# Batch 0 of a packed-attention and top-1 expert kernel: softmax work shared by VectorE and GpSimd, half of the keys loaded through ScalarE's queue, and new conditions on when second-layer weight casts, weight packs and the last softmax steps may go

## The chip, the cores and the metric

The kernel runs on one core of a Trainium2 chip. The metric is device time of one launch in microseconds (us), the median of several runs; smaller is better. TensorE (PE) does the matrix products, VectorE (DVE), ScalarE (ACT) and GpSimd (POOL) the rest, and SyncE (SP) asks for most transfers.

## The reference, cut to what matters

```python
scale = 1.0 / np.sqrt(q.shape[-1])                 # q, k, v: 8 x 8 x 576 x 64, p: 8 x 8 x 32 x 64
p_packed = sm_attn(p, k, v)                        # 32 packed rows for each head
out = sm_attn(q, p_packed, p_packed)               # softmax over 32 columns
x = out.transpose(0, 2, 1, 3).reshape(B, S, 512)
for b in range(B):
    prev_e = -1
    for s in range(S):
        fresh_e = argmax(x[b, s] @ w_gate)
        e = fresh_e if s == 0 or sigmoid(x[b, s] @ w_local) < 0.5 else prev_e
        prev_e = e
        h = np.maximum(x[b, s] @ w1[e], 0.0)       # w1: 8 x 512 x 1024
        out[b, s] = p[e] * (h @ w2[e])             # w2: 8 x 1024 x 512
```

## The kernel before

There are eight batches. For each one the kernel computes 32 packed rows for every head (scores L447 and L508, exponentials L556, their transposes L567, the product with the values L598), and then, for all 576 rows, the second softmax and the two expert layers. The result of the second attention is never formed: the packed rows are multiplied into w1 first ("pack", L1076), and the softmax of the queries is the moving operand of layer 1 (L1104). Which expert a batch uses is only known after its gate products (L922, L930) and a chain on VectorE (L937, L945, L948, L952, L957) that ends in an expert number (L852); SyncE reads it and then asks for that expert's w1 (two transfers of 1 MB into `w1t`, L1026) and w2 (L1033).

Everything is fp32 split into a high and a low part, so that three products replace one. The high part of a packed weight is a cast on ScalarE (`wph`, L1085), the low part a subtraction on VectorE (`wpl`, L1088). The softmax has `a2h` (L788, ScalarE) and its rest `a2l` (L797); w2 has a cast on ScalarE (L1132) and a rest on GpSimd (L1136), both in `w2s`; the hidden layer has a relu on ScalarE (L1115) and a rest on VectorE (L1119). Layer 1 takes eight chunks of 128 hidden columns, c0 to c7, and for each chunk two parts of the 576 rows, of 256 and of 320. A block is six L1104 products for one part of a chunk, followed by six L1156 products of layer 2 for the same part; L1162 and L1166 take the last 64 rows.

Batch 0 is special ("early" in the code). Its keys and queries come in whole transfers (`load_whole`, L291), and its softmax is made by `first_queries`, in two halves of the columns, z = 0 (256 columns) and z = 1 (320 columns), for two row groups Q0 and Q1. A half goes: transposes (L749), maximum (L755), subtraction (L760), exponential (L762), sum (L767), a small addition (L769), reciprocal (L771), product (L773), transposes back into `a2t` (L781), cast (L788), rest (L797). Until there is enough other work PE runs products on zeros (L227) to stay busy.

The order of the program is not written down. A planner at build time (`weave`) holds threads (loads, scores, packs, splits, softmax, gates) and a main thread with the two layers. It carries an estimate of every engine's time, and at each step it lets the first thread go whose inputs it believes to be ready. Each engine then runs its instructions in that fixed order. A changed condition in batch 0 therefore moves instructions of later batches too, because estimates and the planner's credit differ from there on.

Of the kernel before, what the change touches and what calls it, by code (L numbers as in the profile page):

```python
# [14 lines left out]
ALU = mybir.AluOpType  # L15
# [5 lines left out]
NP = 32  # L21
DM, F, E = 512, 1024, 8
HQ = 4
NQ = H // HQ
NG, NM = 6, 3
# [147 lines left out]
def packed_attn_moe_kernel(  # L173
# [12 lines left out]
    nc = tc.nc  # L186
# [4 lines left out]
    clock = Clock()  # L191
    at_batch = [-1]

    def tile_(shape, dtype, name, tag=None):
        bufs = BUFS.get(tag or name, 2)
        x = sb.tile(shape, dtype, name=name, tag=tag or name, bufs=bufs)
        clock.follow(x.tensor.name, tag or name, bufs)
        return x
# [82 lines left out]
        ready.banks = banks  # L281
        return ready

    def load_whole(src, b):

        x = tile_([128, NG, NM * 2 * D], F32, "raw", "qn")
        clock.edges[x.tensor.name] = (H * HALF // 2,)
        clock.rate = 400.0
        rows = src[b].rearrange("h s d -> (h s d)").rearrange("(p g x) -> p g x", p=128, g=NG)
        for z in (slice(0, NG // 2), slice(NG // 2, NG)):  # L290
            nc.sync.dma_start(out=x[:, z], in_=rows[:, z])  # L291
        return x

    def load_values(src, b, Q, x=None, most=True, ends=True):
# [44 lines left out]
    def load_packs_whole(b, queue):  # L339

        x = tile_([128, NQ, 2, D], F32, "p_in")
        clock.rate = 200.0
        queue.dma_start(out=x[:, :, 0], in_=at(p, b).rearrange("(g h) n d -> (h n) g d", g=NQ))
        return x
# [9 lines left out]
    def loads(st):  # L354

        b = st["b"]
        if st["early"]:
            st["p"] = load_packs_whole(b, nc.sync)
            nc.scalar.activation(out=spare_col, in_=ones_col, func=AF.Exp)
            order = (("k", 0), ("t", 0), ("v", 0), ("v", 1), ("w", 0), ("q", 0))  # L360
        else:
            if isinstance(b, int):
                yield need(when=lambda: "loaded" in sts[b - 1] and (b < 2 or "ereg" in sts[b - 2]) and (b <= FIRST or len(sts[b - 2].get("w2", ())) == NC))
            order = (("e", 0), ("p", 1), ("k", 1), ("v", 0), ("v", 1), ("q", 1)) if st["whole"] else (("v", 0), ("v", 1), ("p", 1), ("k", 1), ("q", 1))
        ends = None
        for name, Q in order:
# [27 lines left out]
            x = {"k": k, "v": v, "q": q}[name]  # L394
# [325 lines left out]
    def first_queries(st):  # L720
# [12 lines left out]
        sT, sf, mx, sm = [], [], [], []  # L733
        for lo, hi, room in parts:
            sT.append(tile_([128, NQ, 2, hi - lo, NP], F32, "sT0", room))
            sf.append(sT[-1].rearrange("a q r m n -> a (q r m) n"))
            n = NQ * 2 * (hi - lo)
            mx.append(tile_([128, n], F32, f"mx{n}"))
            sm.append(tile_([128, n], F32, f"sm{n}"))

        def wide(z, x):
            return x[z].unsqueeze(2).broadcast_to([128, sf[z].shape[1], NP])
# [20 lines left out]
            st["raised"] += 1  # L763

        def shared(z):
            yield need(sT[z])
            nc.vector.reduce_sum(out=sm[z], in_=sf[z], axis=AX.X)  # L767
            yield need(sm[z])
            nc.vector.tensor_scalar(out=sm[z], in0=sm[z], scalar1=1e-9, scalar2=None, op0=ALU.add)  # L769
            yield need(sm[z])  # L770
            nc.vector.reciprocal(out=sm[z], in_=sm[z])  # L771
            yield need(sm[z])
            nc.vector.tensor_tensor(out=sf[z], in0=sf[z], in1=wide(z, sm), op=ALU.mult)  # L773

        def returned(z):
            lo, hi, _ = parts[z]
            cols = slice(64 * lo, 64 * hi)
            yield need(sT[z])
            for Q in range(NQ):
                for r in range(2):  # L780
                    nc.vector.transpose(  # L781
                        out=st["a2t"][Q][:, cols].rearrange("a (m r) -> a r m", r=2)[:, r],
                        in_=sT[z][:, Q, r].rearrange("a m n -> a (m n)"),
                    )
                if Q == NQ - 1:
                    st["back" if z == 0 else "returned"] = True
                yield need(st["a2t"][Q][:, cols])
                nc.scalar.copy(out=st["a2h"][Q][:, cols], in_=st["a2t"][Q][:, cols])  # L788
            st["cast"] = True
            give(sT[z])  # L790
# [15 lines left out]
        yield from turned(1, (0,))  # L806
        yield from shared(0)
        yield from returned(0)
        yield from rest(0, (nc.vector, nc.vector))
        yield from turned(1, (1,))  # L810
        yield from highest(1)
        yield from raised(1)
# [235 lines left out]
    def pack_weights(st):  # L1048

        st["wp"], st["packed"], early = [], 0, st["early"]  # L1050
        for fh in range(2):
            yield need(when=lambda: len(st.get("w1", ())) > fh and (
                (st["seconds"] > 2 if early else st["firsts"] > 0) if fh else not early or st["raised"] > 0
            ))
            pieces = st["w1"][fh]
            yield need(slot=("wph", "wpl"))
# [6 lines left out]
            for n, w1t in enumerate(pieces):  # L1063
# [3 lines left out]
                    yield need(w1t)  # L1067
                    yield from look_for_strays()
                if early:
                    yield need(when=lambda: st["asked"] >= 512 * fh + width * (n + 1) and (n == 0 or st["seconds"] > 0))  # L1070
                yield need(w1t, banks=NQ, skip=skip, left=1)
                ts = [bank(skip=skip) for Q in range(NQ)]
                for Q in range(NQ):
# [66 lines left out]
    def splits(st):  # L1140

        for c in range(NC):
            yield need(slot="w2s", when=lambda: len(st.get("w2", ())) > c and st["firsts"] > (c if st["early"] else c - 3))
            yield need(st["w2"][c])
            yield from split(st, c, 2 if st["early"] and c < FRONT else 1)

# [319 lines left out]
```

## Time and profile before

| quantity | value |
|---|---|
| runs | 411.37, 412.01, 412.96 us, median 412.01 |
| profiled execution | 413.25 us, of which the span from first to last instruction is 411.5 us |
| granted TensorE clock, mean | 0.998 |
| PE busy | 401.1 us, 97% of the span |
| DVE, ACT, POOL busy | 248.1, 187.7, 110.9 us |

The span is the stretch from the first to the last instruction; 1.75 us of the profiled execution lie around it. PE is busy nearly all the time, and the last 11.5 us hold 6.00 us of PE work, with the clock at 0.92 of full speed. In the rows below a number in brackets is idle time of that engine just before the instruction, with what ended it.

### The profile page before, as it was taken

What the parts mean: (1) busy time and instruction counts of PE and PEld (TensorE: products, weight loads), DVE (VectorE), ACT (ScalarE), POOL (GpSimd) and SP (SyncE); (2) the same over time, 40 slices, a digit from 0 to 9 for tenths busy, and PEclk for the clock granted to TensorE, in tenths of its full rate; (3) what the DMA queues carried; (4) which work ended last, traced back from release to release, by engine and by line L of the source; (5) the groups of instructions that cost most, each with busy time, mean ns of one, the idle gap of its engine ahead of it and who ended that gap; (6) DMA issues with size and microseconds to landing.
All of it is one profiled execution on the core that took longest, in us unless ns stands there. A gap on an engine that the chain in (4) does not pass through costs nothing.

```text
span 411.5 us, 9811 instructions
## 1 busy us (share of the span) xinstructions
PE 401.1 (97%) x3726; PEld 318.7 (77%) x3727; DVE 248.1 (60%) x665; ACT 187.7 (46%) x447; POOL 110.9 (27%) x139
## 2 busy tenths in 40 slices
PE   8999999999999999999999999999989999999994
PEld 6766777787787888678887887778868788778883
DVE  3678778673986668568944697248843586332221
ACT  2565535653346533475344643545335643453121
POOL 1024502621064203044304411323303423143000
PEclk9999999999999999999999999999999999999999
DMA  7889589965799199659996994899165102921102
GB/s 231 244 309 246 91 210 357 158 163 131 270 231 241 26 218 183 220 192 211 192 317 204 193 193 142 310 210 213 64 243 168 51 14 64 346 70 48 53 0 68
DMA packets 161053, 72.98 MB, mean 177 GB/s; under 512 B 131186, under 2 KB 139882, under 8 KB 161002
## 3 DMA queue, kind: packets, MB, share of 16 engines
q1 hardware_dynamic: 160858, 72.19, 67.8%
q8 instruction: 30, 0.49, 0.5%
q14 instruction: 21, 0.17, 0.1%
q10 hardware_dynamic: 144, 0.13, 0.1%
HBM read 62.87 MB, written 9.44 MB: 176 GB/s over the span
## 4 chain that ended last, share of the span: by engine, by line
PE 89%; DVE 4%; DMA 3%; ACT 1%; issue 1%; SPq 1%; POOL 0%; DVEq 0%; ACTq 0%
PE bank L1156 42%; PE bank L1104 24%; PE bank L1076 4%; PE bank L1162 4%; PE bank L1166 3%; PE bank L598 2%; PE bank L567 2%; PE bank L647 2%; DMA w2raw<-in_moe_w_dram 2%; DMA w1t<-in_moe_w_dram 2%; PE bank L227 2%; PE bank L922 1%; PE bank L439 1%; PE bank L508 1%; PE bank L616 1%
## 5 line engine op out<-in xcount | busy, mean ns | idle before, releaser
L1156 PE MATMUL bank<-w2s,h 128*128 128x512 f32 (+1 forms) x771 | 203.8, 397 | 0.2 <-POOL w2s L1136 0.2
L1156 PEld LDWEIGHTS bank<-w2s,h 128*128 128x128 f32 x771 | 136.2, 188 | 31.1 <-issue 7.8
L1136 POOL TENSOR_TENSOR w2s<-w2raw,w2s 128x512 fp32r<-128x512 f32 (+1 forms) x68 | 84.6, 1258 | 140.0 <-ACT w2s L1132 118.2
L1119 DVE SCALAR_TENSOR_TENSOR h<-bank,h 128x256 fp32r<-128x256 f32 x192 | 61.8, 350 | 94.3 <-ACT h L1115 93.5
L1115 ACT ACTIVATE h<-bank 128x320 fp32r<-128x320 f32 (+1 forms) x128 | 52.9, 413 | 102.9 <-PE bank L1104 100.0
L1104 PEld LDWEIGHTS bank<-a2h,wph 128*128 128x128 f32 x256 | 46.1, 188 | 17.8 <-issue 3.8
L1104 PE MATMUL bank<-a2h,wph 128*128 128x256 f32 (+1 forms) x256 | 56.9, 303 | 0.1
L1104 PE MATMUL bank<-a2h,wpl 128*128 128x256 f32 (+1 forms) x256 | 55.1, 295 | 1.1 <-DVE wpl L1088 1.1
L1104 PE MATMUL bank<-a2l,wph 128*128 128x256 f32 (+1 forms) x256 | 55.2, 296 | 0.0
L1104 PEld LDWEIGHTS bank<-a2h,wpl 128*128 128x128 f32 x256 | 41.1, 188 | 1.5 <-DVE wpl L1088 1.5
L1104 PEld LDWEIGHTS bank<-a2l,wph 128*128 128x128 f32 x256 | 41.0, 188 | 0.3
L710 POOL TENSOR_TENSOR a2l<-a2t,a2h 128x320 fp32r<-128x320 f32 (+1 forms) x26 | 20.7, 819 | 73.5 <-ACT a2h L704 73.5
L1132 ACT CAST w2s<-w2raw 128x512 fp32r<-128x512 f32 x64 | 39.0, 620 | 1.4 <-DMA w2raw<-in_moe_w_dram 1.3
L1088 DVE TENSOR_TENSOR wpl<-bank,wph 128x512 fp32r<-128x512 f32 (+1 forms) x34 | 21.2, 650 | 21.2 <-ACT wph L1085 21.1
L1085 ACT CAST wph<-bank 128x512 fp32r<-128x512 f32 (+1 forms) x34 | 17.4, 565 | 27.4 <-PE bank L1076 27.2
L1162 PE MATMUL bank<-w2s,h 128*128 128x512 f32 x64 | 26.5, 414 | 0.0
L1166 PE MATMUL bank<-w2s,h 128*64 128x512 f32 x64 | 25.2, 393 | 0.0
L1197 ACT ACTIVATE o<-bank,pe 128x512 f32<-128x512 f32 x23 | 15.5, 698 | 9.3 <-PE bank L1156 9.3
L634 DVE STREAM_TRANSPOSE qn<-qn 128x1152 f32<-128x1152 f32 x14 | 19.1, 1366 | 0.0
L1076 PE MATMUL bank<-w1t,ppT 64*32 64x512 f32 x240 | 16.4, 601 | 1.1 <-DMA w1t<-in_moe_w_dram 1.1
L556 ACT ACTIVATE a<-a,nb 128x576 f32<-128x576 f32 x14 | 11.0, 786 | 13.3 <-DVE nb L536 13.3
L1162 PEld LDWEIGHTS bank<-w2s,h 128*128 128x128 f32 x64 | 12.0, 188 | 6.0 <-issue 2.2
(150 smaller groups left out, 387.2 us busy)
## 6 DMA issues: line engine op xcount, KB each, us to landing
w2raw<-in_moe_w_dram SPq DMA_DIRECT2D x64, 256.0 KB, 7.5
w1t<-in_moe_w_dram SPq DMA_DIRECT2D x15, 1024.0 KB, 5.1
kv<-in_v_dram SPq DMA_DIRECT2D x16, 560.0 KB, 8.7
qn<-in_q_dram SPq DMA_DIRECT2D x28, 288.0 KB, 4.3
out_dram<-o SPq DMA_DIRECT2D x31, 256.0 KB, 2.9
qn<-in_k_dram SPq DMA_DIRECT2D x24, 288.0 KB, 4.3
raw<-in_k_dram SPq DMA_DIRECT2D x4, 576.0 KB
raw<-in_q_dram SPq DMA_DIRECT2D x2, 576.0 KB
```

What stands on the lines that cost most here:

```text
L634: nc.vector.transpose(out=qT, in_=qT)
L710: engine.tensor_tensor(out=a2l[:, cols], in0=a2t[:, cols], in1=a2h[:, cols].bitcast(F32), op=ALU.subtract)
L1076: nc.tensor.matmul(out=ts[Q][32 * h:32 * h + 32, :width], lhsT=st["ppT"][Q][rows, 32 * h:32 * h + 32], rhs=w1t[rows, h], start=True, stop= ...
L1088: nc.vector.tensor_tensor(out=lo[:, Q, cols], in0=ts[Q][:, :width], in1=hi[:, Q, cols].bitcast(F32), op=ALU.subtract,)
L1104: nc.tensor.matmul(out=t[:, :width], lhsT=st["wp"][c // 4][wi][:, Q, fs], rhs=a2[ai][Q][:, ts], start=(n == 0), stop=(n == 5),)
L1115: nc.scalar.activation(out=h[:, :n], in_=t[:, :n], func=AF.Relu)
L1119: nc.vector.scalar_tensor_tensor(out=h[:, dst:dst + z - a], in0=t[:, a:z], scalar=0.0, in1=h[:, a:z].bitcast(F32), op0=ALU.max, op1=ALU.su ...
L1132: nc.scalar.copy(out=w[:, 0], in_=raw)
L1136: rest.tensor_tensor(out=w[:, 1, cols], in0=raw[:, cols], in1=w[:, 0, cols].bitcast(F32), op=ALU.subtract)
L1156: nc.tensor.matmul(out=acc[:, cols], lhsT=hs[hi], rhs=w[:, wi, cols], start=(c == 0 and n == 0), stop=(n == 2 and (c == NC - 1 or c == NC ...
L1162: nc.tensor.matmul(out=acc, lhsT=h[:, EDGE:EDGE + 2 * TAIL], rhs=w[:, 0], start=(c == 0), stop=False, skip_group_check=True,)
L1166: nc.tensor.matmul(out=acc[0:TAIL], lhsT=h[:, EDGE:EDGE + TAIL], rhs=w[:, 1], start=False, stop=(c == NC - 1), skip_group_check=True,)
```

## The change

It has five parts. The first half of batch 0's keys is asked for on ScalarE's queue, and the second half stays on SyncE's. In softmax half z = 0 the product is split: VectorE makes Q0's and GpSimd Q1's, and the planner's clock is told that the tile has two regions; the transposes of a row group then wait for that group only, and Q0's rest goes to GpSimd. The sum and what follows it in half z = 1 wait until more than 512 packed columns are done. The second of the early weight packs waits for two layer-1 blocks instead of one layer-2 block, and in the other batches the second half's pack waits for two chunks instead of one. The w2 casts of batch 0 are released by layer-2 progress from c2 on, and c0's by the softmax cast.

```diff
     def load_whole(src, b, queues=(nc.sync, nc.sync)):
...
-        for z in (slice(0, NG // 2), slice(NG // 2, NG)):
-            nc.sync.dma_start(out=x[:, z], in_=rows[:, z])
+        for queue, z in zip(queues, (slice(0, NG // 2), slice(NG // 2, NG))):
+            queue.dma_start(out=x[:, z], in_=rows[:, z])
...
             st["p"] = load_packs_whole(b, nc.sync)
+            st["rawk"] = load_whole(k, b, (nc.scalar, nc.sync))
             nc.scalar.activation(out=spare_col, in_=ones_col, func=AF.Exp)
-            order = (("k", 0), ("t", 0), ("v", 0), ("v", 1), ("w", 0), ("q", 0))
+            order = (("t", 0), ("v", 0), ("v", 1), ("w", 0), ("q", 0))
...
             sT.append(tile_([128, NQ, 2, hi - lo, NP], F32, "sT0", room))
+            clock.edges[sT[-1].tensor.name] = (2 * (hi - lo) * NP,)
...
         def shared(z):
-            yield need(sT[z])
+            yield need(sT[z], when=lambda: z == 0 or st["packed"] > 512)
             nc.vector.reduce_sum(out=sm[z], in_=sf[z], axis=AX.X)
...
-            nc.vector.tensor_tensor(out=sf[z], in0=sf[z], in1=wide(z, sm), op=ALU.mult)
+            if z:
+                nc.vector.tensor_tensor(out=sf[z], in0=sf[z], in1=wide(z, sm), op=ALU.mult)
+                return
+            n = sf[z].shape[1] // NQ
+            for Q, engine in enumerate((nc.vector, nc.gpsimd)):
+                rows, w = slice(n * Q, n * Q + n), wide(z, sm)
+                engine.tensor_tensor(out=sf[z][:, rows], in0=sf[z][:, rows], in1=w[:, rows], op=ALU.mult)
 
         def returned(z):
...
-            yield need(sT[z])
             for Q in range(NQ):
+                yield need(sT[z][:, Q])
                 for r in range(2):
...
-        yield from rest(0, (nc.vector, nc.vector))
+        yield from rest(0, (nc.gpsimd, nc.vector))
...
             yield need(when=lambda: len(st.get("w1", ())) > fh and (
-                (st["seconds"] > 2 if early else st["firsts"] > 0) if fh else not early or st["raised"] > 0
+                (st["seconds"] > 2 if early else st["firsts"] > 1) if fh else not early or st["raised"] > 0
             ))
...
                 if early:
-                    yield need(when=lambda: st["asked"] >= 512 * fh + width * (n + 1) and (n == 0 or st["seconds"] > 0))
+                    yield need(when=lambda: st["asked"] >= 512 * fh + width * (n + 1) and (n == 0 or st["firsts"] > 1))
...
         for c in range(NC):
-            yield need(slot="w2s", when=lambda: len(st.get("w2", ())) > c and st["firsts"] > (c if st["early"] else c - 3))
+            yield need(slot="w2s", when=lambda: len(st.get("w2", ())) > c and (
+                (st["firsts"] > c if c < 2 else st["seconds"] > c - 2) if st["early"] and c else "cast" in st if st["early"] else st["firsts"] > c - 3
+            ))
```

The change moves instructions. Lines of the changed kernel are one larger from L291 on, two larger around L749 to L762, eight larger around L797 to L1136, and ten larger from L1156 on.

On GpSimd the first place is the work of batch 0 after its last preparation for the scores. Before, the w2 rests of c0 to c3 came in halves, then c4, and then the softmax rest of half z = 1 for Q0 (`a2l`):

```order
L493 MEMSET a_473 128x4
L1136 TENSOR_TENSOR w2s<-w2raw,w2s 128x256 x8
L1136 TENSOR_TENSOR w2s<-w2raw,w2s 128x512
L797 TENSOR_TENSOR a2l<-a2t,a2h 128x320
L1136 TENSOR_TENSOR w2s<-w2raw,w2s 128x512 x2
L493 MEMSET a_723 128x4
L1136 TENSOR_TENSOR w2s<-w2raw,w2s 128x512
```

After it, softmax work of half z = 0 leads, and the rest of half z = 1 for Q0 stands behind all the w2 rests:

```order
L494 MEMSET a_473 128x4
L781 TENSOR_TENSOR sT_417<-sT_417,sm_419 128x256
L805 TENSOR_TENSOR a2l<-a2t,a2h 128x256
L1144 TENSOR_TENSOR w2s<-w2raw,w2s 128x256 x8
L1144 TENSOR_TENSOR w2s<-w2raw,w2s 128x512 x4
L805 TENSOR_TENSOR a2l<-a2t,a2h 128x320
```

On ScalarE at the end of batch 0, from the softmax casts of half z = 1 on, `a` holds the scores of batch 1 and `a1T` their transposes. Before:

```order
L788 CAST a2h<-a2t 128x320
L1115 ACTIVATE h<-bank_665 128x256
L1132 CAST w2s<-w2raw 128x512
L556 ACTIVATE a_473,s_691<-a_473,nb 128x576
L1115 ACTIVATE h<-bank_680 128x256
L1132 CAST w2s<-w2raw 128x512
L1115 ACTIVATE h<-bank_741 128x256
L569 COPY a1T<-bank_770 116x384
L569 COPY a1T<-bank_775 116x256
L556 ACTIVATE a_723,s_784<-a_723,nb 128x576
L965 ACTIVATE ex<-under 128x40
L967 ACTIVATE fresh_all<-lt 128x5
```

After; the relu of the first 320-row block (`bank_759`) and both exponentials now stand ahead of all copies of `a1T`:

```order
L1123 ACTIVATE h<-bank_694 128x256
L796 CAST a2h<-a2t 128x320
L1140 CAST w2s<-w2raw 128x512
L796 CAST a2h<-a2t 128x320
L1123 ACTIVATE h<-bank_759 128x320
L557 ACTIVATE a_473,s_784<-a_473,nb 128x576
L557 ACTIVATE a_741,s_786<-a_741,nb 128x576
L570 COPY a1T<-bank_790 116x384
L570 COPY a1T<-bank_795 116x256
L570 COPY a1T<-bank_806 116x384
L973 ACTIVATE ex<-under 128x40
```

The second place is the border between batches 2 and 3, first on PE, up to the pack (`w1t`) that needs batch 3's expert. Before:

```order
L1156 MATMUL bank_2318<-w2s,h 128x512 x3
L1162 MATMUL bank_2324<-w2s,h 128x512
L1166 MATMUL bank_2324<-w2s,h 64x512
L1104 MATMUL bank_2553<-a2h,wph 128x320 x2
L1104 MATMUL bank_2553<-a2h,wpl 128x320 x2
L1104 MATMUL bank_2553<-a2l,wph 128x320 x2
L567 MATMUL bank_2562<-ident,a_2492 116x128 x3
L567 MATMUL bank_2568<-ident,a_2492 116x128 x2
L1156 MATMUL bank_2311<-w2s,h 128x512 x3
L1156 MATMUL bank_2318<-w2s,h 128x512 x3
L1076 MATMUL bank_2591<-w1t,ppT 32x512 x4
L1076 MATMUL bank_2592<-w1t,ppT 32x512 x4
```

After; the six layer-1 and six layer-2 products between the scores of batch 4 (L508, now L509) and the pack are gone from there:

```order
L1166 MATMUL bank_2307<-w2s,h 128x512 x3
L1166 MATMUL bank_2314<-w2s,h 128x512 x3
L509 MATMUL bank_2546<-qn,p_in 32x288 x4
L509 MATMUL bank_2547<-qn,p_in 32x288 x4
L509 MATMUL bank_2556<-qn,p_in 32x288 x4
L509 MATMUL bank_2557<-qn,p_in 32x288 x4
L1172 MATMUL bank_2319<-w2s,h 128x512
L1176 MATMUL bank_2319<-w2s,h 64x512
L568 MATMUL bank_2581<-ident,a_2540 116x128 x3
L568 MATMUL bank_2586<-ident,a_2540 116x128 x2
L1084 MATMUL bank_2595<-w1t,ppT 32x512 x4
L1084 MATMUL bank_2596<-w1t,ppT 32x512 x4
```

Further ahead, the six layer-1 products of one block and three of layer 2 now stand before the gate products (L922, now L930), where they had stood behind them. On VectorE, from the transpose of the gate's result (`lt`) to the expert's number (`e`). Before:

```order
L937 STREAM_TRANSPOSE lt<-bank_2403 128x160
L945 TENSOR_REDUCE gmx<-lt 128x5
L948 TENSOR_TENSOR under<-lt,gmx 128x40
L460 STREAM_TRANSPOSE qn<-qn 128x4x288
L1119 SCALAR_TENSOR_TENSOR h<-bank_2424,h 128x256
L1119 SCALAR_TENSOR_TENSOR h<-bank_2424,h 128x64
L952 SCALAR_TENSOR_TENSOR vc<-under,code 128x40
L957 TENSOR_REDUCE codes_all<-vc 128x5
L852 TENSOR_SCALAR e_2457<-codes_all 1x1
```

After; one more pair of hidden-layer rests and the transpose of `p_in`, which stood ahead of the gate before, now lie between:

```order
L945 STREAM_TRANSPOSE lt<-bank_2414 128x160
L1127 SCALAR_TENSOR_TENSOR h<-bank_2399,h 128x256
L1127 SCALAR_TENSOR_TENSOR h<-bank_2399,h 128x64
L953 TENSOR_REDUCE gmx<-lt 128x5
L461 STREAM_TRANSPOSE qn<-qn 128x4x288
L956 TENSOR_TENSOR under<-lt,gmx 128x40
L1127 SCALAR_TENSOR_TENSOR h<-bank_2445,h 128x256
L1127 SCALAR_TENSOR_TENSOR h<-bank_2445,h 128x64
L960 SCALAR_TENSOR_TENSOR vc<-under,code 128x40
L423 STREAM_TRANSPOSE p_in<-p_in 128x256
L965 TENSOR_REDUCE codes_all<-vc 128x5
L860 TENSOR_SCALAR e_2468<-codes_all 1x1
```

## Rows read from the trace of the kernel before

**Rows 1.** The page's busy times: us, share of the span, instructions.
```profile
PE 401.1 (97%) x3726; PEld 318.7 (77%) x3727; DVE 248.1 (60%) x665; ACT 187.7 (46%) x447; POOL 110.9 (27%) x139
```

**Rows 2.** Timeline of the first 8 us: start, duration, engine, line, operation.
```profile
1.31 4.63 PE L227 MATMUL bank<-warm 128*128 128x256 f32 x10 [1.31 <-DVE warm L220]
...
1.38 0.94 SPq L291 DMA_DIRECT2D raw<-in_k_dram  x2
```

**Rows 3.** Timeline, 24.5 to 29 us: first softmax half.
```profile
25.06 0.69 DVE L773 TENSOR_TENSOR sT<-sT,sm 128x512 f32<-128x512 f32 x1
```

**Rows 4.** Timeline, 29 to 40 us: two layers of batch 0.
```profile
34.19 0.43 PE L1156 MATMUL bank<-w2s,h 128*128 128x512 f32 x1
...
36.14 1.09 PE L1076 MATMUL bank<-w1t,ppT 64*32 64x512 f32 x16
...
37.16 1.65 PE L1156 MATMUL bank<-w2s,h 128*128 128x512 f32 x6
...
38.65 0.40 PE L1104 MATMUL bank<-a2h,wph 128*128 128x256 f32 x2
...
39.69 0.38 PE L1104 MATMUL bank<-a2h,wpl 128*128 128x256 f32 x1 [0.52 <-DVE wpl L1088]
```

**Rows 5.** Waits of PE, whole span: engine, line, waited for, total, times, longest.
```profile
PE bank L1104 <- DVE wpl L1088: 1.1, 2, 0.6
PE bank L1076 <- DMA w1t<-in_moe_w_dram: 1.1, 1, 1.1
```

**Rows 6.** Timeline, 42 to 52 us: GpSimd beside VectorE, end of batch 0.
```profile
42.24 2.79 POOL L1136 TENSOR_TENSOR w2s<-w2raw,w2s 128x512 fp32r<-128x512 f32 x2
42.32 1.56 DVE L797 TENSOR_TENSOR a2l<-a2t,a2h 128x320 fp32r<-128x320 f32 x1
...
46.60 0.71 PE L567 MATMUL bank<-ident,a 128*116 128x128 f32 x5
...
47.06 0.54 PE L1104 MATMUL bank<-a2h,wph 128*128 128x320 f32 x2
...
49.32 0.75 ACT L569 COPY a1T<-bank 116x384 f32<-116x384 f32 x2
...
51.41 0.96 PE L1156 MATMUL bank<-w2s,h 128*128 128x512 f32 x3
```

**Rows 7.** Timeline, 161 to 178 us: from batch 3's gate to its first layer.
```profile
161.54 0.43 DVE L422 STREAM_TRANSPOSE p_in<-p_in 128x256 f32<-128x256 f32 x1
...
162.29 0.65 PE L922 MATMUL bank<-a2t,gate 128*32 128x128 f32 x16
...
165.34 0.39 PE L1162 MATMUL bank<-w2s,h 128*128 128x512 f32 x1
...
165.80 0.46 PE L1104 MATMUL bank<-a2h,wph 128*128 128x320 f32 x2
...
166.68 0.86 PE L1156 MATMUL bank<-w2s,h 128*128 128x512 f32 x3
...
167.35 1.01 SPq L1026 DMA_DIRECT2D w1t<-in_moe_w_dram  x2
167.41 0.56 DVE L1119 SCALAR_TENSOR_TENSOR h<-bank,h 128x256 fp32r<-128x256 f32 x2 [0.73 <-ACT h L1115]
...
167.47 1.20 PE L508 MATMUL bank<-qn,p_in 64*32 64x288 f32 x32
...
169.51 0.78 ACT L556 ACTIVATE a<-a,nb 128x576 f32<-128x576 f32 x1 [2.13 <-DVE nb L536]
...
172.79 1.09 PE L1076 MATMUL bank<-w1t,ppT 64*32 64x512 f32 x16
...
177.52 0.39 PE L1104 MATMUL bank<-a2h,wpl 128*128 128x256 f32 x1 [0.62 <-DVE wpl L1088]
```

**Rows 8.** Tile w1t: time from issue of its DMA to landing.
```profile
DMA to landing us min/median/max: 5.0/5.1/5.1
```

**Rows 9.** Chain that ended last, 296 to 310 us: start, duration, link.
```profile
300.47 6.80 DMA w1t<-in_moe_w_dram
```

More of the change, by code (lines that the diff above doesn't have):

```diff
@@ L282, in need, with load_whole @@
         return ready
-    def load_whole(src, b):
+    def load_whole(src, b, queues=(nc.sync, nc.sync)):
         x = tile_([128, NG, NM * 2 * D], F32, "raw", "qn")
```

## The prediction

> **What bounds the kernel now.** I read the share of busy time first: PE is busy for 401.1 of 411.5 us [rows 1]. A step that moves work between the other engines can therefore give back only what PE loses, so the second view was PE's waits, of which two matter here [rows 5]: 1.1 us for `wpl` in two places, at 39.69 [rows 4] and 177.52 [rows 7], and 1.1 us for one transfer of `w1t`. Third came the timeline at four places: the start, the first half of the softmax, the end of batch 0, and the border to batch 3. The orders of before and after say what stands where; every duration below is from the trace. Names of lines are those of before. The sum is made on the profiled execution (413.25 us, 1.24 above the median); the difference is then put on the median of 412.01.
>
> **The keys.** ScalarE's queue asks for the first half, which SyncE did in one of two issues that take 0.94 together [rows 2], so 0.47 each. Until 5.94 PE runs its warm products (1.31 + 4.63), whose number is unchanged. They cover an earlier landing completely, and a landing 0.47 later would still be hidden or cost that much. I take 0, with ends 0 and +0.4.
>
> **First softmax half.** VectorE's product of 512 elements took 0.69 [rows 3]. For 256 the bounds are half of that, 0.35, and all of it; I take 0.4, since fixed costs don't halve. GpSimd made two rests of 512 in 2.79 [rows 6], so for 256 I take a quarter of that, 0.7. Both instructions have two inputs in SBUF, and how two such get on when they overlap is seen in the same rows: VectorE's rest of 320 took 1.56 beside the two of GpSimd, although VectorE needed only 0.69 for 512. It ended when GpSimd was half through: VectorE seems to have got nowhere until GpSimd had ended one. So I let one wait for the other: VectorE 25.06 to 25.46, GpSimd to 26.2. Q0's transposes and cast come 0.3 earlier, Q1's at the time they had. Layer 1 starts with Q0 and then needs Q1, so c1 comes 0.3 earlier: -0.3, with ends -0.6 (no wait) and 0 (GpSimd goes first).
>
> The Trainium skill ("SBUF — State Buffer", Who interferes with whom) says that a VectorE instruction with two such inputs and a GpSimd instruction that reads there exclude each other for their whole length. The row above agrees. If the two shared instead, the start of batch 0 would come out 0.3 better than I take.
>
> **Second pack, second half.** The second early pack now stands ahead of layer 2 of c0, so layer 2 waits less for the w2 rests. Six L1156 take 1.49 undisturbed (37.16 to 38.65), but 1.95 in c2 (34.19 to 36.14) [rows 4]: 0.46 to be had. The sum of half z = 1 now comes behind both `wpl` subtractions, which before were parted by transposes; that takes about half of the 0.52 wait at 39.69, say 0.25. So PE passes that place 0.3 + 0.46 + 0.25 = 1.0 earlier.
>
> I expect all of it to be given back. GpSimd now makes the rests of c4 to c7, at 2.79 / 2 = 1.4 each [rows 6], before the softmax rest of Q0. The cast of c7 stands behind c7's relu and a softmax cast on ScalarE. Following the order with these prices, c7's rest ends at about 45.4, and Q0's, 0.9 (320 of 512 by 1.4), at 46.3, or at 46.7 if VectorE's rest of Q1 gets in first. PE begins the first 320-row block at 47.06 [rows 6] less 1.0, less 0.5 for the transposes L567 that no longer precede it (46.60 to 47.06), so at about 45.5; it needs that rest after four of its six products (0.88 by 165.80 to 166.68 [rows 7], so 0.6), at 46.1. That is a stall of 0.2 to 0.6. Behind it ScalarE does in a row the relu (0.4), two exponentials (0.78 [rows 7] and 0.2 for reading the sum, each) and the copies of `a1T` (0.75 for a pair [rows 6], twice, and 0.4 for two small steps between). From 46.7 to 47.1 this gives 51.4 to 51.8 for the last copy, and the values' last products 0.2 more. Layer 2 of c7, at 51.41 before, comes at 51.6 to 52.0. The start-up as a whole: **+0.3**, with ends -1.3 (the lead of 1.0 and the 0.3 of sharing kept) and +0.6.
>
> **Border to batch 3.** Before, the gate products begin at 162.29, the weights are asked for at 167.35, and the pack that needs them starts at 172.79, without a wait: 5.06 and 10.50 after the gate [rows 7]. A landing of 5.1 [rows 8] leaves 0.3. Now one layer-1 block and three layer-2 products stand before the gate; the like of them takes 1.67 (165.80 to 167.47). The pair L1162 and L1166 (0.46, 165.34 to 165.80) comes ahead of the pack. So PE's own work from gate to pack falls to 10.50 - 1.67 + 0.46 = 9.3. On VectorE the way to the expert number grows by the transpose of `p_in` (0.43) and a pair of hidden rests (0.56) [rows 7], from 5.06 to 6.05 until the request. The weights land at 6.05 + 5.1 = 11.15 after the gate: 1.85 of waiting. The exponential alone would take 1.3 of it: the scores L508 (1.2) begin at 9.3 less 0.46 for the transposes L567, 0.46 for the pair and 1.2, so at 7.2; the exponential ends 3.0 later (169.51 + 0.78 + 0.2 - 167.47), and the transposes follow, so the pack can't start before 10.6. Behind the pack the second `wpl` was there after 4.73 (172.79 to 177.52) because a transpose stood between the two; it still does, so I take 4.5. From gate to that place: 11.2 + 4.5 = 15.7 where it was 15.23, and the gate itself is 1.67 later: **+2.1**. Ends: +0.2, if transfer and exponential were hidden (9.3 in place of 11.2), and +3.8, if the transfer takes 6.80 as before batch 6 [rows 9].
>
> **Later batches.** In batch 6 the request went out at 300.47, the weights came 6.80 later [rows 9], and PE waited 1.1 [rows 5]. By the order, the pack is 2.0 earlier there (one layer-1 block, three layer-2 products and a pair less ahead of it), and the gate too, by six layer-2 products (about 1.5). So the wait changes little: -1.1 if the transfer takes 5.1, +0.6 if 6.80; I take -0.3. In batches 1, 2, 4, 5 and 7 the same count leaves room between landing and pack: 0.
>
> **Sum**: 0 (keys) + 0.3 + 2.1 - 0.3 = +2.1. On the profiled execution that is 415.35, on the median **414.1 us**. What a measurement here can tell from no change is 0.5%, 2.06 us: faster is under 409.95, slower over 414.07. My forecast lies at the upper border.
>
> **The rivals.**
> - *The weights of batch 3 come in time for the rest of PE's work* (other work moved ahead of the pack covers the exponential, or the transfer is quicker). The loss there is then between 0.2 and half of the forecast's, 1.1, and the sum 0.3 + 0.2 - 0.3 = +0.2 up to +1.1: 412.2 to 413.1. For it: 5.0 to 5.1 is what the tile's view gives for the landings, so the transfer itself need not get longer. Against it: the exponential alone costs 1.3, and nothing is left between it and the pack. 0.22.
> - *Faster: the lead of batch 0 stays.* If GpSimd ends c7's rest by 45.2, Q0's rest (0.9) is ready at 46.1, when PE wants it, and the 1.3 remains; with batch 6's wait gone (-1.1) and batch 3 covered (+0.2), -2.2, so 409.8. For it: 45.2 is only 0.2 before the time worked out above. Against: four rests of 1.4 follow one another, c7's cast is not free before PE has finished that chunk, and the exponentials still stand behind the relu. 0.14.
> - *Slower: the transfer of batch 3 takes 6.80.* Then batch 3 costs 3.8: 0.3 + 3.8 - 0.3 = +3.8, 415.8, and 416.7 where batch 6 loses its 0.6 as well. For it: 6.80 was measured when the two transfers and w2's were in flight. Against: in batch 3 before, they landed within 5.4. 0.17.
> - *The change does nothing for PE*: order shifts only, 412.0; this is in the first rival's place, and in its chance.
>
> **How the numbers follow.** The forecast has 0.47, with its own range 413.1 to 415.1; about half of that lies over 414.07. Faster: 0.12 from the second rival. Slower: 0.24 from the forecast and 0.17 from the third rival, 0.41. Within 0.5%: the rest, 0.47. The range leaves out the lower half of the second rival and the upper half of the third: 410.2 to 416.0.
>
> **What would show it.** In the profile after: c1's first layer at about 28.0 and the first `wpl` wait of PE gone or halved; layer 1 of the first 320-row block waiting for GpSimd's `a2l`; L567 waiting for the exponential of `a`, and layer 2 of c7 at 51.6 to 52.0; about 2 us of PE waiting at batch 3's pack, named by the transfer of `w1t` or by L556, where the border has no wait now; batch 6's wait between 0 and 1.7. The prediction is wrong if the first 320-row block is passed without a wait (then the start-up is a gain), or if batch 3's pack starts less than 10.5 after its gate.

## The result, and the profile after

The changed kernel is slower: 416.64 us as the median of 18 runs (413.56 to 419.67), against 412.5 us for the kernel before in 18 runs (411.37 to 416.93). The ratio is 1.0096 with a 95% interval of [1.0070, 1.0121], so 3.96 us (the medians differ by 4.1). The forecast was +2.1 and 414.1 us: the direction held, the size was about half of what came, and the median lies 0.6 us outside the range. The profiled execution of the changed kernel took 415.32 us with a span of 413.6, so it shows only 2.1 of the 3.96. Its runs lie 6 us apart, and one profile is one draw from that spread; the experiments had to settle the rest. Of the executions reported below, the first of e8 (418.85 us), with its profile, and one of e3 (2196 us) were disturbed and are left out.

From the page of the changed kernel, the busy times, the row of the w2 casts on ScalarE (what follows the second bar is the idle time before them and what ended most of it), and the DMA issues of `w2raw` (KB each, us to landing):

```profile
PE 402.2 (97%) x3726; PEld 318.7 (77%) x3727; DVE 251.4 (61%) x665; ACT 188.0 (45%) x447; POOL 112.2 (27%) x140
...
L1140 ACT CAST w2s<-w2raw 128x512 fp32r<-128x512 f32 x64 | 39.4, 620 | 4.3 <-DMA w2raw<-in_moe_w_dram 3.9
...
w2raw<-in_moe_w_dram SPq DMA_DIRECT2D x64, 256.0 KB, 8.0
```

The same two rows from the page of the kernel before:

```profile
L1132 ACT CAST w2s<-w2raw 128x512 fp32r<-128x512 f32 x64 | 39.0, 620 | 1.4 <-DMA w2raw<-in_moe_w_dram 1.3
...
w2raw<-in_moe_w_dram SPq DMA_DIRECT2D x64, 256.0 KB, 7.5
```

PE is still busy 97% of the time [rows 1]. New is that ScalarE's casts stood idle for 3.9 us in front of transfers, 1.3 before. The forecast used neither of the two rows of before.

The waits of PE in the changed kernel (total, times, longest):

```profile
PE bank L568 <- ACT a L557: 1.1, 1, 1.1
...
PE bank L1084 <- DMA w1t<-in_moe_w_dram: 0.8, 2, 0.6
PE bank L1112 <- POOL a L494: 0.7, 1, 0.7
PE bank L930 <- DVE a2t L789: 0.6, 2, 0.4
PE bank L1166 <- ACT h L1123: 0.4, 1, 0.4
```

Three of the five stood in the forecast: the exponential and the transfer at the border, and GpSimd's late rest of Q0 (named by the MEMSET that follows it on GpSimd). Two did not: PE waiting for `h` (the relu) in batch 0, and the gate products of batch 0 waiting 0.6 for the transposes of softmax half z = 1, a little ahead of GpSimd's late rest. The timeline of the changed kernel, batch 0:

```profile
23.97 0.57 SPq L1041 DMA_DIRECT2D w2raw<-in_moe_w_dram  x1
...
24.57 0.42 DVE L781 TENSOR_TENSOR sT<-sT,sm 128x256 f32<-128x256 f32 x1
...
24.69 0.78 POOL L781 TENSOR_TENSOR sT<-sT,sm 128x256 f32<-128x256 f32 x1 [7.53 <-DVE sm L773]
...
32.00 0.62 ACT L1140 CAST w2s<-w2raw 128x512 fp32r<-128x512 f32 x1 [2.00 <-DMA w2raw<-in_moe_w_dram]
...
32.53 0.73 ACT L764 ACTIVATE sT<-sT 128x640 f32<-128x640 f32 x1
...
33.17 0.64 ACT L1123 ACTIVATE h<-bank 128x256 fp32r<-128x256 f32 x2
...
33.59 1.66 PE L1166 MATMUL bank<-w2s,h 128*128 128x512 f32 x6 [0.42 <-ACT h L1123]
...
38.22 0.62 ACT L1140 CAST w2s<-w2raw 128x512 fp32r<-128x512 f32 x1 [0.84 <-DMA w2raw<-in_moe_w_dram]
38.27 0.18 PEld L1112 LDWEIGHTS bank<-a2h,wpl 128*128 128x128 f32 x1 [0.27 <-DVE wpl L1096]
...
47.49 0.56 PE L1112 MATMUL bank<-a2l,wph 128*128 128x320 f32 x2 [0.67 <-POOL a L494]
...
52.16 1.19 PE L1166 MATMUL bank<-w2s,h 128*128 128x512 f32 x4
```

The cast of c3's w2 comes to the head of ScalarE at 30.0, stands there until its weights land at 32.0, 8 us after their request, and holds the softmax exponential and two relus behind it. Layer 2 then waits 0.42 for `h`. At 38.22 the cast of c4 also starts late, by 0.84, but in this profile PE does not wait for it. Layer 2 of c7 ends this stretch at 52.16 where it was at 51.41 [rows 6]: 0.75 later.

In the kernel before, c3's weights were asked for at 24.62, and ScalarE came to their cast only at 33.97, 9.4 us later, and did not wait:

```profile
24.62 0.37 SPq L1033 DMA_DIRECT2D w2raw<-in_moe_w_dram  x1
...
33.97 0.61 ACT L1132 CAST w2s<-w2raw 128x512 fp32r<-128x512 f32 x1
```

ScalarE's order says why the cast now comes sooner. Before, each cast of c2 to c5 had a relu or more between it and the next one:

```
L1132 CAST w2s (c2) / L1115 relu / L1132 CAST w2s (c3) / L762 exponential / L1115 relu
L1132 CAST w2s (c4) / L1115 relu / L1132 CAST w2s (c5)
```

After, the new condition in `splits` (`seconds > c - 2`) lets two casts go in a row, c3's ahead of the relus of c2 and c3, and c5's ahead of those of c4 to c6:

```
L1140 CAST w2s x2 (c2, c3) / L764 exponential / L1123 relu / L1123 relu
L1140 CAST w2s x2 (c4, c5) / L1123 relu / L1123 relu / L1123 relu
```

The timeline of the changed kernel at the border to batch 3:

```profile
164.60 0.64 PE L930 MATMUL bank<-a2t,gate 128*32 128x128 f32 x16
...
170.42 1.01 SPq L1034 DMA_DIRECT2D w1t<-in_moe_w_dram  x2
...
174.61 0.81 PE L568 MATMUL bank<-ident,a 128*116 128x128 f32 x5 [1.09 <-ACT a L557]
...
176.00 1.68 PE L1084 MATMUL bank<-w1t,ppT 64*32 64x512 f32 x16 [0.58 <-DMA w1t<-in_moe_w_dram]
```

The request is 5.82 after the gate (forecast 6.05), the pack 11.40 after it (forecast 11.2), held first by the exponential and then by the transfer, 1.67 in all. The pack itself took 1.68 where it took 1.09 before [rows 7]. The stretches below show the clock: it averaged 0.66 of full speed over the second of them, and from 177 to 179 it stood at the lower of its two levels (1.2 GHz, where full speed is 2.4). Each row has the span of the stretch, then the busy time of each engine, the granted clock, the DMA share and GB/s:

```profile
170.00:175.00 5.00, 3.91 (x46) 2.23 (x45) 4.10 (x14) 1.31 (x3) 0.46 (x4) 1.00 0.69 208
175.00:180.00 5.00, 4.42 (x77) 2.49 (x79) 3.17 (x7) 3.25 (x8) 0.00 (x0) 0.66 1.05 394
```

### The profile page after: what moved, and what is told of

The parts are those of the page before. It is cut to its first block, busy times and chain, and to the rows that moved or that the text cites. A ratio compares the mean times of both kernels' runs of the same rounds, so it can differ in the third digit from the quotient of the medians.

```text
span 413.6 us, 9823 instructions
## 1 busy us (share of the span) xinstructions
PE 402.2 (97%) x3726; PEld 318.7 (77%) x3727; DVE 251.4 (61%) x665; ACT 188.0 (45%) x447; POOL 112.2 (27%) x140
## 4 chain that ended last, share of the span: by engine, by line
PE 88%; DMA 5%; DVE 2%; POOL 1%; issue 1%; ACT 1%; SPq 0%; POOLq 0%; DVEq 0%; ACTq 0%
PE bank L1166 41%; PE bank L1112 23%; PE bank L1172 4%; PE bank L1084 4%; PE bank L1176 3%; DMA w2raw<-in_moe_w_dram 3%; DMA w1t<-in_moe_w_dram 3%; PE bank L599 3%; PE bank L568 2%; PE bank L648 2%; PE bank L227 2%; PE bank L509 1%; PE bank L440 1%; POOL w2s L1144 1%; PE bank L930 1%
## 5 line engine op out<-in xcount | busy, mean ns | idle before, releaser
L1112 PE MATMUL bank<-a2h,wph 128*128 128x256 f32 (+1 forms) x256 | 56.0, 299 | 0.1
```

The source lines that it names most:

```text
L1112: nc.tensor.matmul(out=t[:, :width], lhsT=st["wp"][c // 4][wi][:, Q, fs], rhs=a2[ai][Q][:, ts], start=(n == 0), stop=(n == 5),)
```

## The experiments

The kernel's planner decides the order anew at every step, so undoing one line moves everything behind it. In most of the kernels below, a recorded list of the planner's steps, of one of the two kernels, takes the place of its choice:

```diff
-            x = the planner's choice among the steps that are ready
+            x = the next step of the recorded list (from a batch on)
```

The instructions are the same; the list holds the order fixed and one thing is changed in it. Their line numbers differ from those above by the inserted code. Ratios are to the kernel before, timed beside it.

**Which half of the program.** e1 is the changed kernel again. e2 has its batch 0 and then the order of before; e3 the start of before and then the changed order.

> The changed kernel once more, to see a second profile and the spread of its times. In the first profile it was 2.1 us over the kernel before, but its median over 18 runs was 4.1 over, with runs from 413.6 to 419.7. Theory M (two fixed losses: batch 0 about +0.8, border to batch 3 about +2.7, given back about 1.3 in batch 6): the second profile shows the same two places with the same sizes, and runs vary by under 1.5 us. Theory C (the border's idle time lets TensorE's clock fall to its lower level, and for how long varies): the border costs between 2 and 6 us from run to run, the start does not vary. Theory D (batch 0 now waits for transfers of w2, whose landing varies): the start costs between 0 and 4 us from run to run.

> Batch 0 of the changed kernel; from batch 1 on the planner takes its steps in the order of the kernel before. Theories M and C: the border to batch 3 is as before, without a wait for the weights and at full clock, so only the start is left: +0.5 to +1.0 us over before, spread as before (under 1.5 us without outliers). Theory D: +0.5 to +4 us, spread of 4 us or more.

> Batch 0 of the kernel before; from batch 1 on the order of the changed kernel. Theory M: +2.7 at the border less 1.1 to 1.4 in batch 6, so +1.3 to +1.6 us, spread under 1.5 us. Theory C: +1.3 to +5 us, median about +3, spread of 4 us or more, and the profile shows a granted clock under 0.8 behind batch 3's pack. Theory D: +1.3 to +1.6 us, little spread.

Measured: e1 416.46 us, 1.0094 [1.0080, 1.0109]; e2 414.65, 1.0041 [1.0023, 1.0059]; e3 414.17, 1.0033 [1.0022, 1.0045]. Both parts cost: 1.7 us by the start, 1.4 by the rest. The forecast had 0.3 and 1.8. The timeline of e1 in batch 0 has the same two casts waiting, longer than in the first profile:

```profile
32.89 0.62 ACT L1140 CAST w2s<-w2raw 128x512 fp32r<-128x512 f32 x1 [2.78 <-DMA w2raw<-in_moe_w_dram]
...
34.47 1.66 PE L1166 MATMUL bank<-w2s,h 128*128 128x512 f32 x6 [1.28 <-ACT h L1123]
...
39.73 1.37 ACT L1140 CAST w2s<-w2raw 128x512 fp32r<-128x512 f32 x2 [1.46 <-DMA w2raw<-in_moe_w_dram]
```

**The border's clock.** e4 is the changed kernel with warm products on zeros where the border waits: the first line below two times before batch 4's score transposes, the second once before batch 3's pack.

```diff
+  nc.tensor.matmul(out=tp[:, :256], lhsT=warm[:, :128], rhs=warm, start=True, stop=True)
+  nc.tensor.matmul(out=ts[0][:, :256], lhsT=warm[:, :128], rhs=warm, start=True, stop=True)
```

> The changed kernel in its own order, with three products on zeros (each 256 columns, about 0.46 us) put where TensorE is idle at the border: two ahead of the first transposes of batch 4's scores, one ahead of batch 3's pack. Their results are overwritten by what follows. Theory C: the clock stays at its upper level, the pack takes 1.1 us in place of 1.7, the border costs 0.5 to 1 us less, the spread falls under 1.5 us and the median to about +2. Theories M and D: the same time as the changed kernel within 0.3 us, and the same spread.

Measured: 415.9, 1.0067 [1.0049, 1.0085]; the clock stays at 1.00 and the pack takes 1.09. But e1, unfilled, has that too in the same stretch:

```profile
175.00:180.00 5.00, 3.61 (x86) 2.31 (x88) 4.10 (x13) 4.06 (x10) 0.00 (x0) 1.00 1.04 396
```

and its four executions, at mean clocks of 0.993 to 0.999, took 416.32 to 416.84 us. So the fall to 0.66 does not come in every execution. From the gate to the values (L599) the first profile took 14.26, e1 12.95 and the kernel before 12.73. Of the 1.31 between the first two, 0.42 is the transfer, for which the pack waited 0.58 there and 0.16 in e1; the clock has about 0.9. But e1 loses the full 0.94% without a fall at the border in its profile. The 0.27% between e1 and e4 is hardly more than their intervals.

**The casts.** e5 moves only c3's cast back behind the relu. e6 has batch 0 of the changed kernel with the old condition of `splits` (and of the pack outside batch 0), then the order of before. e10 is e5 with c7's cast and rest also put behind the rest of Q0. e13 leaves the casts and asks for c3's weights ahead of w1's 1 MB.

```diff
 e5, e10: splits(c3) behind relu(c2); e10 also splits(c7) behind rest(Q0)
 e6:  -  (st["firsts"] > c if c < 2 else st["seconds"] > c - 2) if st["early"] and c else ...
      +  st["firsts"] > (c if st["early"] else c - 3)
 e13: -  if c == FRONT - 1:
      +  if c == FRONT:
```

> The changed kernel with one instruction moved on ScalarE: the w2 cast of c3 stands behind the softmax exponential of z = 1 and the relu of c2 (as before the change) and no longer ahead of them. All else is the order of the changed kernel. Theory D1 (this cast waits for its transfer until 32.0 to 33.3 and holds exponential and relu, and so PE, behind it): the wait of layer 2 for h at 33 to 35 is gone; 0.4 to 1.6 us less than the changed kernel, median +2.2 to +3.0 over before. Theory D2 (the casts of c4 and c5, which wait until 38 to 41, hold as much): under 0.5 us less, and layer 2 of c4 still waits. Theory C (clock at the border sets the spread): no change.

> Batch 0 of the changed kernel, but with the old condition for the w2 casts, so that casts and relus alternate; from batch 1 on the order of the kernel before. Beside the run with the new start and the old rest (1.0041). Theory D (casts waiting for transfers are the loss of batch 0): 1.5 us or more comes back, -0.5 to +0.4 us against before, spread as before. Rival (the loss is GpSimd's order and the late rest of Q0): +0.8 to +1.8 us, as with the new condition.

> The changed kernel with the cast of c3 behind the relu of c2 and, besides, c7's w2 cast on ScalarE and its rest on GpSimd moved behind the softmax casts and the rest of Q0 of half z = 1. Theory P (as predicted: the late rest stalls the first 320-row block, which holds exponentials and copies behind it): the wait of that block is gone, 0.5 to 0.8 us less than with the cast of c3 alone (1.0059), so 1.0040 to 1.0047. Rival (the exponentials behind the relu set the end of batch 0 anyway): under 0.3 us less.

> The changed kernel with one request moved on SyncE: c3's quarter MB of w2 is asked for ahead of the second half of w1 (1 MB), no longer behind it. Every other order is that of the changed kernel. Theory D1 (ScalarE's cast of c3 stands at the transfer, and exponential, relu and PE behind it): c3's cast no longer waits or waits under 0.8 us, layer 2 of c2 no longer waits for h, 0.8 to 1.6 us less than the changed kernel (1.0095), so 1.0055 to 1.0075. Rival (it was the place of the cast in the order, not its transfer): no change.

Measured: e6 412.9, 1.0001 [0.9988, 1.0014]; compared with e2, the old condition returns 0.40%, 1.65 us, the whole loss of the start. But the planner ordered the rest of batch 0 anew in e6, on PE, VectorE and GpSimd too, and GpSimd's late rest no longer stalls PE there, so e6 alone doesn't single out the casts. e5 415.49, 1.0059 [1.0037, 1.0082]; e10 415.18, 1.0051 [1.0028, 1.0075]; e13 415.61, 1.0085 [1.0056, 1.0115]. One cast alone doesn't do it: in e5 c3's cast no longer waits, but c4's then stands 1.84 at its transfer and PE 0.66 for the relu; in e10 the stall of the first 320-row block is gone, but c4's cast waits 2.07 and PE 1.6 for `h`; in e13 the pair c4, c5 waits 1.03. e13 missed its expectation (1.0055 to 1.0075): its profile, of 415.06 us, shows PE waiting only 0.3 for `h`, so what its slower runs lose isn't seen in it.

**The other edits of the start.** e9 is the changed kernel with both halves of the keys asked for by SyncE. e11 is the kernel before with nothing but the first softmax half split between the engines; e12 adds the changed order of the later batches (from batch 4 on).

```diff
 e9:  -  load_whole(k, b, (nc.scalar, nc.sync))
      +  load_whole(k, b, (nc.sync, nc.sync))
 e11: +  the edits of shared, returned, rest(0, ...) and clock.edges, no other
```

> The changed kernel in its own order, but both halves of batch 0's keys are asked for by SyncE again. Theory K0 (as predicted: hidden, 0): the same median as the changed kernel within 0.4 us. Theory K+ (the split brings the scores 0.3 to 0.7 us earlier when the keys land early, as four profiles show, and up to 1.4 later when the second half lands late, as two do): the median moves by under 0.5 us, but the scores of batch 0 start at 9.0 to 9.4 and the spread becomes smaller by 1 us or more.

> The kernel before with one part of the change alone: in half z = 0 the product is shared by VectorE and GpSimd, and Q0's rest goes to GpSimd; from batch 1 on the old order. As predicted: layer 1 starts 0.3 us earlier and little of it is lost later, 0 to -0.5 us against before. Rival: the lead is lost again to the w2 transfers, which land when they land: 0.

> The part above together with the changed order from batch 4 on (0.9985 by itself). If both add up: 0.4 to 1.1 us faster than before, 0.9973 to 0.9990. If GpSimd's part of the half meets the port of VectorE at a bad time, no better than 0.9985.

Measured: e9 415.49, 1.0067 [1.0043, 1.0092]; e11 413.2, 1.0016 [1.0000, 1.0032]; e12 412.8, 1.0004 [0.9985, 1.0022]. The keys' 0.29% against the changed kernel is not resolved, and the casts wait in e9 as they did (2.87, PE 1.4 for `h`). The split of the softmax half makes nothing faster by itself, and e11 and e12 both came out slower than expected.

**The border and the later batches.** e14 is the changed kernel with the order of before in batches 1 to 3. e7, and e16 again, have the order of before up to batch 3 and the changed one from batch 4. e8 joins e6 and e7; e15 undoes the keys, c3's cast and the border.

> The changed kernel with the old order in batches 1 to 3, and its own from batch 4 on. Theory M (the border costs 2.0 us whatever the start): 1.0045 to 1.0055. Rival (start and border are not independent: a later start hides part of the border's wait or makes it longer): 1.0065 or more, or 1.0035 or less.

> The kernel before up to batch 3, the changed order from batch 4 on. Theory M (border to batch 3 costs about 2, batch 6 gives back): faster than before by 0.4 to 1.1 us, the wait of batch 6's pack for w1t gone or under 0.3. Against the old start with the whole new rest (1.0033) this is 1.8 to 2.4 us less, which is the border alone. Rival (no gain in batch 6; the 1.0033 is all spread over later batches): same as before within 0.3 us, or slower.

> The kernel before up to batch 3 and the changed order from batch 4 on, once more, since its interval (0.9969 to 1.0001) reached no change. If batch 6's wait is the gain: 0.9975 to 0.9995 again, in one piece with the first, and no wait of a pack for w1t of over 0.3 us. Rival: 1.0000 within 0.0010, the first was chance.

> The parts that seem good together: batch 0 of the changed kernel with the old condition for the casts, batches 1 to 3 in the old order, from batch 4 on the new order. The sum of the two runs before this one: -0.3 to -1.4 us against before if both theories hold.

> The changed kernel with three things undone: keys both asked for by SyncE, the cast of c3 behind the relu of c2, and batches 1 to 3 in the old order. By the single runs these cost 0.27%, 0.36% and 0.48%: 1.0095 less 0.0111 is 0.9984, about the run with the old order until batch 3 alone. If it stays at 1.0020 or more, a fourth loss is left in batch 0 (GpSimd's late rest of Q0, 0.7 us in the profile).

Measured: e14 414.84, 1.0060 [1.0036, 1.0083]; e7 412.22, 0.9985 [0.9969, 1.0001]; e16 412.81, 1.0000 [0.9983, 1.0017]; e8 413.61, 1.0009 [0.9990, 1.0027], where I had expected a gain; e15 415.37, 1.0051 [1.0033, 1.0070]. e14, less than the changed kernel's 1.0096 by 0.36%, puts the border at 1.5 us, with an uncertainty nearly as large. The gain that e7 seemed to show from batch 4 on did not come back in e16, so no version is shown to beat the kernel before. e15 missed: I had expected it near the kernel before, at 0.9984, and it kept 2.1 us. Its profile named what was left: with c3's cast moved, c4's waited 2.84 for its transfer and PE 2.2 for the relus.

**Two instructions.** That gave the last test. e18 is e2 again. e17 is e2 with two casts of ScalarE moved, c3's behind c2's relu and c5's behind its own, and nothing else on any engine.

```diff
-CAST c2, CAST c3, exponential, relu c2, relu c3 ... CAST c4, CAST c5, relu, relu, relu
+CAST c2, exponential, relu c2, CAST c3, relu c3 ... CAST c4, relu, relu, CAST c5, relu
```

> New batch 0, old order from batch 1 on, and two instructions moved on ScalarE: the w2 cast of c3 behind the relu of c2, and that of c5 behind the relu of c5, so that no two casts stand in a row ahead of relus. Theory D (pairs of casts that wait for their transfers are the loss of batch 0): the wait for h is gone at c2 and under 0.8 at c4, 1.0 to 1.6 us less than the next run, so 1.0000 to 1.0020. Theory D' (c4's cast alone, still ahead of its relu and waiting 1 to 3 us for its transfer, keeps most of the loss): 1.0025 to 1.0040. Rival (GpSimd's late rest of Q0 and what stands behind it): 0.2 us less at most.

> The new batch 0 with the old order from batch 1 on, unchanged, for a comparison on one chip in one piece: 1.0041 the first time, so 1.0025 to 1.0055, and in the profile waits of layer 2 for h at c2 or c4 of 0.5 to 2 us together.

Measured on the same chip: e18 415.08, 1.0046 [1.0025, 1.0067]; e17 413.25, 1.0005 [0.9986, 1.0024]. Two instructions of 0.62 us, each moved back by two places on its engine, are worth 0.41%, 1.7 us; the intervals do not overlap. In e17's profile the late rest of Q0 still stalls PE by 0.64, so that stall alone is not the loss. The timeline of e18 (L1337 is the cast, L1320 the relu):

```profile
24.42 0.36 SPq L1238 DMA_DIRECT2D w2raw<-in_moe_w_dram  x1
...
36.05 0.62 ACT L1337 CAST w2s<-w2raw 128x512 fp32r<-128x512 f32 x1 [4.25 <-DMA w2raw<-in_moe_w_dram]
...
37.21 0.64 ACT L1320 ACTIVATE h<-bank 128x256 fp32r<-128x256 f32 x2
...
37.63 2.74 PE L1363 MATMUL bank<-w2s,h 128*128 128x512 f32 x6 [2.74 <-ACT h L1320]
```

Here c3's weights landed 11.6 us after their request, and PE lost 2.74 at once. Behind this wait the clock fell as at the border (the stretch from 37 to 42, as above):

```profile
37.00:42.00 5.00, 4.37 (x23) 2.05 (x24) 0.76 (x2) 0.95 (x4) 1.16 (x2) 0.66 1.16 232
```

The layer-2 block took 2.74 where it took 1.66 in the changed kernel, and the pack behind it 1.53 where it took 1.09: about 1.5 us more. In the profiles of the changed kernel, e1, e2 and e4 the clock stood at 1.00 from 24 to 47. The timeline of e17 (cast L1368, relu L1351):

```profile
23.68 0.45 SPq L1269 DMA_DIRECT2D w2raw<-in_moe_w_dram  x1
...
33.76 0.36 ACT L1351 ACTIVATE h<-bank 128x256 fp32r<-128x256 f32 x1
...
34.86 0.62 ACT L1368 CAST w2s<-w2raw 128x512 fp32r<-128x512 f32 x1 [0.74 <-DMA w2raw<-in_moe_w_dram]
...
41.17 0.62 ACT L1368 CAST w2s<-w2raw 128x512 fp32r<-128x512 f32 x1 [3.21 <-DMA w2raw<-in_moe_w_dram]
```

c3's weights are as late, 11.2 us after the request, but the relu stands ahead of the cast, and the relu is what PE's layer 2 wants. c4's cast, which was not moved, still waits 3.21, and PE 1.5 for `h`; this profile, of 414.81 us, is one of the slower runs of e17 (412.41 to 416.58). The waits for `h` are 0.28 at c2 and 1.23 at c4, so of what I expected the time came, but not the profile without these waits; how the faster runs look isn't seen.

## Why the prediction was right and wrong

**The step that failed** is the start-up term of +0.3 (ends -1.3 and +0.6). The runs put it at 1.7 and 1.9 (e2, e18). In its working, "the rest of Q0" on GpSimd was the only thing that could be late; ScalarE's casts were counted as so many microseconds in a queue. That a cast moved ahead of relus stands there until its weights land was not looked at, though the page before gave a landing of 7.5 us and the order shows two casts in a row. c3's weights were asked for at 24.0, so 31.5 was to be expected by that row, against a cast that ScalarE now reaches at 30.0. e17 shows it, and e6 agrees: with the old place of two of the casts, no loss of the start can be measured any more. The spread fits it: in the six profiles with this order of batch 0 (e2, the changed kernel, e14, e1, e4, e18) c3's weights landed at 31.8, 32.0, 32.2, 32.9, 33.3 and 36.1, and PE's waits for `h` were 0.8, 0.4, 0.6, 1.5, 2.3 and 2.7 us. Spans compare only where the later batches are in one order too: e2 and e18, the same program, have 411.8 and 415.3. That the landing makes most of the spread of the changed kernel's 18 runs is likely but not shown, since the others have no profile.

**What held in the start-up.** Layer 1 of c1 came 0.92 earlier (27.34 for 28.26), of which the scores of batch 0, which began 0.60 earlier, explain 0.60; the remaining 0.32 is the forecast's 0.3. From the scores to c1 the profiles took 18.88 on average with the old product (four) and 18.49 with the shared one (fifteen). PE's first `wpl` wait, 0.52 before, is gone from its rows, and that of the weight load there fell from 0.73 to 0.27: "gone or halved". The lead was given back: the stall at the first 320-row block is 0.67 (forecast 0.2 to 0.6) and layer 2 of c7 came at 52.16 (forecast 51.6 to 52.0). But the stall was no large part of the loss: e17 has it, 0.64, and no loss that can be measured. e10, without it, against e5 (1.0051, 1.0059) is too uncertain to price it.

**The first softmax half** came out by luck: the number fits, the reason does not. I let VectorE's and GpSimd's products exclude each other, as the rows on the end of batch 0 suggested [rows 6]. The Trainium skill ("SBUF — State Buffer", Who interferes with whom) says the same of such a pair. Here they overlapped for 0.30 us and took 0.42 and 0.78, and nearly the same in every profile with the shared product; on its own a GpSimd rest of 256 took 0.73. If a product costs GpSimd about what a rest does, neither was blocked, so on this pair the measurement speaks against the rule and against my reading. By that reading's own rival, sharing, c1 should have come 0.6 earlier; it came 0.3 to 0.4 earlier, and why not more is open.

**The keys** were forecast at 0, with ends 0 and +0.4. Over the profiles the scores of batch 0 began at 9.19 on average with the old issue (8.66 to 9.55, eight profiles) and at 9.02 with the new (8.43 to 10.05, eleven profiles): no difference that this spread can show, but the ends were too narrow, since PE waited 1.4 for the keys in e5. The start that was 0.60 earlier in the first profile is one draw from this spread.

**The border** was forecast at +2.1, and its mechanism is borne out: the exponential, then the transfer, hold the pack. The ratios put it at 1.5 (e14) and at 1.4 to 2.0 (e3 less e16 or e7). The profiles, without a fall of the clock, put it at 1.7. In e3, whose start is that of before, PE passes the second `wpl` place at 178.95 for 177.52 [rows 7], 1.43 later, though it ended the last layer-2 block that both have ahead of the gate 0.29 earlier: 1.72. In e1 the two delays are 3.93 and 2.26: 1.67. The term was 0.4 too large. The gate came 1.6 later (forecast 1.67), and from the gate to that place e3 took 15.37 and e1 15.33 (forecast 15.7, before 15.23). Where the clock fell, in the first profile, the border cost 2.6. The transfer of 6.80 of the third rival did not occur: it took 5.58 in the first profile.

**Batch 6**, -0.3, is not resolved by the times: 0.9985 in e7, 1.0000 in e16. The 1.1 that I read there was one draw: with the old order the pack of batch 6 waited 0.8 in e2, 0.5 in e6 and e11, and under 0.2 in e17 and e18. With the new order of the later batches no profile has that wait, but in some of them the pack of batch 7, which I had put at 0, waits for `w1t` instead (0.8 in e14 and e15, under 0.2 in e16).

**The sum.** 1.7 to 1.9 of the start and 1.4 to 2.0 of the rest make 3.1 to 3.9 of the 3.96 measured; the intervals of the single runs, 0.1 to 0.3%, don't close it further, and what share the clock's fall has in the median stays open. The rivals that kept the border free or the lead of batch 0 fell; "slower" was right, but not by the transfer of batch 3.

## What to carry to other kernels

When an instruction that reads a transfer is moved forward on an engine that works in order, compare its new place with the landing of that transfer, request plus the row's time to landing, and then ask what stands behind it: the price is not the instruction's own duration but the wait, paid by every relu or exponential queued there. Where the landing varies from run to run, the loss does too, and a single profile may show little of it; hold the order fixed and move that one instruction. A moved order has as many suspects as instructions, and undoing one edit at a time missed here, because the next cast in line took over the wait.

## What the runs showed of the hardware

A transfer of 256 KB, asked for at 23.5 and at 24.4, landed 8.4 us after its request in the profile of e2 and 11.6 after it in that of e18, two profiles of the same program.

The granted clock did not follow the length of PE's waits from one profile to the next. At the border of the first profile PE waited 1.09 and then 0.58, and the clock fell to its lower level (0.66 on average over 5 us). In e1, with 1.10 and 0.16 at the same place, it stayed at 1.00, but so it did in batch 0 of e17, where PE waited 1.23 and then 0.57. Behind the one wait of 2.74 in e18 it fell.
